# One change to a tuned kernel: the instruction order of its main region is left to the framework's scheduler

## The chip, the cores and the metric

The kernel runs on one core of a Trainium2 chip. The core has five engines that run side by side, each through its own list of instructions in the order of that list, and wait for one another on semaphores: PE (TensorE, matrix products), DVE (VectorE), ACT (ScalarE), POOL (GpSimd) and SP (SyncE, which here issues most of the DMA transfers). The metric is the device time of one execution in microseconds (us); lower is better. The kernel before took 1051.46 us, the median of three runs (1046.29 to 1054.59).

## The reference, cut to what matters

Three layers, one after the other, on 2304 tokens of 512 channels: block-causal attention, a gated feed-forward layer, and a layer of eight experts of which each token uses one.

```python
scores = scale * q @ k.T                          # 4 batches, 8 heads, 576 positions, 64 wide
scores = where(block_i >= block_j, scores, -1e9)  # blocks of 64 positions
attn   = exp(scores - max) / (sum + 1e-9)
x      = merge_heads(attn @ v)                    # 2304 x 512
x      = (sigmoid(x @ w_gate) * (x @ w_val)) @ w_out      # 512 -> 1536 -> 512, weights in float64
logits = x @ g                                    # 2304 x 8
e      = argmax(logits); p = softmax(logits)[e]
out    = p * (relu(x @ w1[e]) @ w2[e])            # per token, 512 -> 1024 -> 512
```

## The kernel before, in words

**Attention.** 4 batches x 4 pairs of heads x 5 query tiles make 80 items. An item goes through PE (scores L254 or L263/L270, masks L276), DVE (row maximum L291/L293), ACT (exp L307/L316), DVE (sum and reciprocal L324, L326, scaling L361), PE (transposes L338/L347 into `ep`), ACT (copy `et` L340), PE (times v, L383), ACT and DVE (the result `x` as a rounded part L391 and a rest L392) and POOL (store to `x_d`, L394). The letters of the strings G, H and QUICK give the order of these steps over neighbouring items. Batch 0 has a form of its own (`quick`), for which k and q are transposed on PE (L217) and copied by ACT and DVE to `qn` (L222) and `kn` (L224).

**Weights.** The feed-forward weights arrive as float64 and are turned on the chip into a rounded float32 part and a rest, in 27 pieces, of which 15 have 128x1024 elements. For each piece SP loads the words into one of three buffers (L556), ACT makes the exponent part (L568), DVE shifts and joins the words (L569, L573, and the add L578), ACT casts to the rounded part (L587) and DVE takes the rest (L589). `weights()` is a generator; before the feed-forward layer starts it is advanced by a pace (FILL) between the letters of the attention strings.

**Feed-forward.** Nine units `u` of 256 tokens, twelve blocks `f` of 128 columns. For each (u, f) PE forms gate and value in `gv` (L652 to L654, 24 matmuls of 256 columns), ACT and DVE form the product (`th` L677/L678, `g` L680/L681), and PE adds `g` times `w_out` to `acc` (L694). Unit u can start when its tokens' attention items have been stored and loaded again (`xu`). The work of units 0 and 1 runs interleaved with the attention of later batches and with the weight pieces; from unit 2 on the attention is fed in by a rate that counts how many steps are needed before the next unit.

**Routing and experts.** Logits are made per unit on PE (L718, L727, L737). The first 16 tiles of 128 tokens are routed while the last unit runs, the last two after it. Routing turns logits into a table of token numbers: matmuls into `pt` (L885), then on DVE `tb`, `ix` and `gi` (L898 to L902). The experts work in slots of 128 tokens: 9 early ones and then up to a total of 20 that are always executed. For a slot POOL gathers the tokens by `gi` (L1008, an indirect DMA), PE transposes them (L1031, `xtp`), ACT and DVE split them (`xt`, L1033/L1034). The expert's weights are four tiles `raw` of 1 MB, loaded by SP (L975/L977) and split by ACT into `eh` (L998) and by DVE into `el` (L999); PE multiplies (L1045, `hp` and `yp`), ACT applies relu and makes `h` (L1056), PE transposes it (L1065), ACT and DVE split it (`ht`, L1067/L1068), ACT scales the result by the gate (L1085) and POOL stores it to the rows of its tokens (L1086).

**What sets the order.** All this is emitted inside one region, `with tc.manual_schedule():` (L1096), in the order that the loops of the region give: the list `msegs` for the feed-forward layer, credits and paces for attention and weights, the strings TICK0 to TICK2 for the slots. In that region every engine gets its instructions in the order in which they are emitted.

Of the kernel before, what the change touches and what calls it, by code (L numbers as in the profile page):

```python
# [24 lines left out]
def attn_moe_moe_kernel(  # L25
# [1067 lines left out]
        )  # L1093


    with tc.manual_schedule():  # L1096
        ag = attention()
        done = [-3]

# [319 lines left out]
```

## Time and profile before

| | before |
|---|---|
| median of 3 runs | 1051.46 us |
| the profiled execution: its time | 1051.92 us |
| its span, first to last instruction | 1050.1 us |
| mean granted TensorE clock | 0.968 |
| PE busy | 957.8 us (91%) |
| DVE busy | 626.0 us (60%) |
| ACT busy | 578.2 us (55%) |
| POOL busy | 128.3 us (12%) |

The span is that of the core's instructions; 1.8 us of the execution lie around it. Busy times are sums over the whole span, and the stages differ: the table of stretches shows each engine's busy time in the part of the span named at the start of the row, with the granted clock of TensorE (1.00 is 2.4 GHz, 0.50 is 1.2 GHz). A wait belongs to the engine named first; behind the arrow stands what ended it.

### The profile page before, as it was taken

The numbers are of one execution on the slowest core, as the hardware profiler recorded it, in microseconds if no ns is written. First come the engines' busy times: TensorE is split into PE (matmuls) and PEld (weight loads), VectorE is DVE, ScalarE is ACT, GpSimd is POOL, SyncE is SP. The second block draws the span as 40 slices with busy tenths as digits, with TensorE's granted clock in tenths as the row PEclk, the third lists the DMA queues.
The fourth block names the chain that finished last, engine by engine and source line by source line (L and its number), as shares of the span: only waits on it lengthen the run. The fifth ranks groups of instructions, "written<-read, shape, count | busy, mean of one in ns | idle before, by whom it ended". The sixth has DMA issues, their size and how long they took to land. (4 is left out here: it accounts for less than half of the span.)

```text
span 1050.1 us, 17803 instructions
## 1 busy us (share of the span) xinstructions
PE 957.8 (91%) x6636; PEld 818.2 (78%) x6636; DVE 626.0 (60%) x1194; ACT 578.2 (55%) x1188; POOL 128.3 (12%) x180
## 2 busy tenths in 40 slices
PE   6776777997879999999999999999989999999994
PEld 3445676886658988888988998999987888888883
DVE  5777887765333444444444432121648999988984
ACT  5665565653534545445454532222238888888884
POOL 1211101111000110100101000000021123122110
PEclk9988989998999999999999999999999999999998
DMA  8546661422342031031130020201262354969110
GB/s 214 165 131 203 191 185 56 121 81 80 118 118 63 16 112 41 23 106 34 30 95 24 14 71 6 66 3 61 87 235 81 116 189 138 334 227 357 47 41 20
DMA packets 114715, 112.91 MB, mean 108 GB/s; under 512 B 62591, under 2 KB 85119, under 8 KB 114624
## 3 DMA queue, kind: packets, MB, share of 16 engines
q1 hardware_dynamic: 106800, 88.90, 27.6%
q0 software_dynamic: 7824, 22.82, 6.4%
q8 instruction: 54, 0.88, 0.3%
q14 instruction: 37, 0.30, 0.1%
HBM read 144.46 MB, written 22.28 MB: 159 GB/s over the span
## 5 line engine op out<-in xcount | busy, mean ns | idle before, releaser
L652 PE MATMUL gv<-xu,w 128*128 128x256 f32 x776 | 229.8, 296 | 6.5 <-ACT w L587 6.0
L653 PE MATMUL gv<-xu,w 128*128 128x256 f32 x776 | 220.6, 284 | 0.0
L654 PE MATMUL gv<-xu,w 128*128 128x256 f32 x776 | 220.6, 284 | 0.0
L999 DVE TENSOR_TENSOR el<-raw,eh 128x2048 fp32r<-128x2048 f32 x84 | 191.6, 2289 | 26.6 <-ACT eh L998 25.2
L694 PE MATMUL acc<-w,g 128*128 128x512 f32 x582 | 163.6, 410 | 4.6 <-ACT x2r L708 2.7
L998 ACT CAST eh<-raw 128x2048 fp32r<-128x2048 f32 x84 | 161.0, 1918 | 3.8 <-DMA raw<-in_moe_w_dram 3.7
L652 PEld LDWEIGHTS gv<-xu,w 128*128 128x128 f32 x776 | 149.6, 193 | 13.1 <-ACT w L587 6.5
L653 PEld LDWEIGHTS gv<-xu,w 128*128 128x128 f32 x776 | 149.7, 193 | 1.1
L654 PEld LDWEIGHTS gv<-xu,w 128*128 128x128 f32 x776 | 149.3, 192 | 0.0
L678 DVE SCALAR_TENSOR_TENSOR th<-th,gv 128x256 f32<-128x256 f32 x108 | 45.2, 418 | 143.4 <-ACT th L677 142.9
L694 PEld LDWEIGHTS acc<-w,g 128*128 128x128 f32 x582 | 102.3, 192 | 23.7 <-ACT x2r L708 3.2
L394 POOL DMA_DIRECT2D x_d<-x x80 | 54.8, 685 | 521.1 <-DVE x L392 350.1
L1045 PE MATMUL hp<-eh,xt 128*128 128x512 f32 x320 | 109.2, 402 | 0.0
L1045 PE MATMUL yp<-eh,ht 128*128 128x512 f32 x320 | 106.1, 393 | 0.7 <-ACT ht L1067 0.7
L677 ACT ACTIVATE th<-gv 128x256 f32<-128x256 f32 x108 | 41.6, 385 | 117.1 <-PE gv L654 116.9
L307 ACT ACTIVATE e<-sp,nm 128x128 f32<-128x128 f32 (+3 forms) x128 | 66.4, 526 | 50.8 <-DVE nm L291 50.5
L680 ACT CAST g<-th 128x256 fp32r<-128x256 f32 x108 | 43.9, 406 | 78.7 <-DVE th L678 75.8
L681 DVE TENSOR_TENSOR g<-th,g 128x256 fp32r<-128x256 f32 x108 | 45.9, 425 | 52.6 <-ACT g L680 52.6
L383 PE MATMUL av<-et,v 128*64 128x128 f32 (+1 forms) x960 | 67.6, 272 | 5.4 <-ACT et L340 5.1
L1045 PEld LDWEIGHTS yp<-eh,ht 128*128 128x128 f32 x320 | 59.9, 188 | 13.5 <-ACT ht L1067 0.9
L338 PE MATMUL ep<-ident,e 128*128 128x128 f32 x320 | 57.0, 285 | 14.5 <-DVE x L392 8.6
L1045 PEld LDWEIGHTS hp<-eh,xt 128*128 128x128 f32 x320 | 60.2, 188 | 11.9
(190 smaller groups left out, 1575.0 us busy)
## 6 DMA issues: line engine op xcount, KB each, us to landing
raw<-in_moe_w_dram SPq DMA_DIRECT2D x88, 1024.0 KB
xu<-x_d SPq DMA_DIRECT2D x36, 256.0 KB
x_d<-x POOLq DMA_DIRECT2D x64, 128.0 KB, 2.3
spare<-in_moe_w_gate_dram SPq DMA_DIRECT2D x10, 512.0 KB
spare<-in_moe_w_val_dram SPq DMA_DIRECT2D x10, 512.0 KB
spare<-in_moe_w_out_dram SPq DMA_DIRECT2D x10, 512.0 KB
x_d<-x2r SPq DMA_DIRECT2D x9, 512.0 KB
k<-in_k_dram SPq DMA_DIRECT2D x32, 128.0 KB
```

What stands on the lines that cost most here:

```text
L307: nc.scalar.activation(out=r["e"][:, j, 0:n], in_=r["view"][:, j, :], func=AF.Exp, bias=r["nm"][:, j:j + 1], accum_out=su[:, j:j + 1],)
L338: nc.tensor.transpose(ep[:, cs], r["e"][:, part, cs], ident)
L383: nc.tensor.matmul(av[hs, 0:m], lhsT=d["v"][:, c, j, :], rhs=rhs, start=(c == 0), stop=(c == t))
L394: nc.gpsimd.dma_start(out=x_d[hp][:, :, t0:t0 + m], in_=x[:, :, 0:m].bitcast(F32))
L652: nc.tensor.matmul(o, lhsT=wh, rhs=x[:, 0, :], start=(kk == 0 and nm == "g"), stop=False, **kw)
L653: nc.tensor.matmul(o, lhsT=wh, rhs=x[:, 1, :], start=False, stop=False, **kw)
L654: nc.tensor.matmul(o, lhsT=wl, rhs=x[:, 0, :], start=False, stop=(kk == KD - 1), **kw)
L681: nc.vector.tensor_tensor(out=g[:, 1, :], in0=th, in1=g[:, 0, :], op=ALU.subtract)
L694: nc.tensor.matmul(o, lhsT=g[:, part, hs], rhs=w_o(w, f), start=(f == fs[0] and w == "h" and part == 0), stop=(f == fs[-1] and part == 1),)
L998: nc.scalar.copy(out=h, in_=raw[j])
L999: nc.vector.tensor_tensor(out=l, in0=raw[j], in1=h, op=ALU.subtract)
L1045: nc.tensor.matmul(o, lhsT=t[:, cs], rhs=w[:, c * 512:(c + 1) * 512], start=(first and c == 0 and part == 0 and w is eh), stop=(last and c ...
```

## The change

One line. The region of fixed order becomes an empty context, and the framework's scheduler chooses the order of the instructions on every engine within what their data allow:

```diff
@@ -1093,7 +1093,7 @@
-    with tc.manual_schedule():
+    with ExitStack():
         ag = attention()
         done = [-3]
```

The instructions are the same ones in the same numbers on each engine, and no tile, buffer or transfer is added or removed. From about 300 to about 750 us PE's order is the same row for row. It differs at three places, which follow. Names are those of the tiles: what is written, an arrow, what is read; a trailing number tells instances of a tile apart (the numbers themselves differ by two between the kernels).

DVE at the start of the program. `kn` and `nm` belong to attention (keys, row maxima), `spare` is the buffer of weight pieces. Before:

```order
L224 COPY kn<-tp 128x576
L291 TENSOR_REDUCE nm<-sp 128x2
L324 TENSOR_SCALAR su<-su 128x2
L326 RECIPROCAL su<-su 128x2
L361 TENSOR_SCALAR e<-e,su 128x128 x2
L291 TENSOR_REDUCE nm<-sp 128x2
L324 TENSOR_SCALAR su<-su 128x2
L326 RECIPROCAL su<-su 128x2
L569 TENSOR_SCALAR spare_105<-spare_102 128x1024
```

Now:

```order
L569 TENSOR_SCALAR spare_105<-spare_102 128x1024
L224 COPY kn<-tp 128x576
L573 SCALAR_TENSOR_TENSOR spare_105<-spare_102,spare_105 128x1024
L578 ISA spare_105<-spare_105,spare_106 128x2048
L291 TENSOR_REDUCE nm<-sp 128x2
L569 TENSOR_SCALAR spare_105<-spare_103 128x1024
L291 TENSOR_REDUCE nm<-sp 128x2
L573 SCALAR_TENSOR_TENSOR spare_105<-spare_103,spare_105 128x1024
L324 TENSOR_SCALAR su<-su 128x2
L578 ISA spare_105<-spare_105,spare_106 128x2048
```

The rounding of weight pieces 0 and 1 moved ahead of the first key copy and the first maxima; on ACT, L568 of both pieces moved ahead of the first exp in the same way. By the 18th write of `x` DVE now has the instructions of about four more pieces in front of it (32 of them instead of 17); by the 24th write the two orders stand level.

PE in the third unit of the feed-forward layer, at the first use of the weights `w17`. Before:

```order
L338 MATMUL ep_2785<-ident_77,e_2698 128x128 x3
L652 MATMUL gv_2814<-xu_948,w17_2796 128x256
L653 MATMUL gv_2814<-xu_948,w17_2796 128x256
L654 MATMUL gv_2814<-xu_948,w17_2796 128x256
L652 MATMUL gv_2814<-xu_948,w17_2796 128x256
```

Now:

```order
L338 MATMUL ep_2783<-ident_77,e_2696 128x128 x3
L338 MATMUL ep_2825<-ident_77,e_2696 128x128 x3
L694 MATMUL acc_1231<-w16_2155,g_2723 128x512 x3
L270 MATMUL sp_2857<-ka_991,qa_989 128x288
L271 MATMUL sp_2857<-ka_991,ql_990 128x288
L270 MATMUL sp_2857<-ka_991,qa_989 128x288
L271 MATMUL sp_2857<-ka_991,ql_990 128x288
L270 MATMUL sp_2857<-ka_991,qa_989 128x288
L271 MATMUL sp_2857<-ka_991,ql_990 128x288
L270 MATMUL sp_2857<-ka_991,qa_989 128x288
L652 MATMUL gv_2812<-xu_946,w17_2794 128x256
```

Transposes, an `acc` part and scores that came behind this block's `gv` now stand ahead of it, and most of the block's other matmuls come 28 rows later.

DVE at the passage to the experts, where the token numbers `gi` of the first slots are made. Before:

```order
L999 TENSOR_TENSOR el_8376<-raw_7514,eh_8375 128x2048
L678 SCALAR_TENSOR_TENSOR th<-th,gv 128x256
L681 TENSOR_TENSOR g<-th,g 128x256
L898 COPY tb<-pt 128x45
L900 SCALAR_TENSOR_TENSOR ix<-tb 128x9
L901 TENSOR_SCALAR ix<-ix 128x9
L902 CAST gi<-ix 128x9
L904 TENSOR_SCALAR em<-tb 128x9
L905 TENSOR_TENSOR si<-em,ix 128x9
L906 TENSOR_TENSOR tb<-tb 128x9
L907 TENSOR_TENSOR gw<-tb 128x9
L999 TENSOR_TENSOR el_8441<-raw_7515,eh_8440 128x2048
```

Now:

```order
L999 TENSOR_TENSOR el_8439<-raw_7513,eh_8438 128x2048
L678 SCALAR_TENSOR_TENSOR th<-th,gv 128x256
L999 TENSOR_TENSOR el_8481<-raw_7514,eh_8480 128x2048
L681 TENSOR_TENSOR g<-th,g 128x256
L678 SCALAR_TENSOR_TENSOR th<-th,gv 128x256
L898 COPY tb<-pt 128x45
L900 SCALAR_TENSOR_TENSOR ix<-tb 128x9
L904 TENSOR_SCALAR em<-tb 128x9
L906 TENSOR_TENSOR tb<-tb 128x9
L901 TENSOR_SCALAR ix<-ix 128x9
L681 TENSOR_TENSOR g<-th,g 128x256
L902 CAST gi<-ix 128x9
```

The second and third `el` of slot 0 moved ahead of `gi`. In the slots that follow, ACT's `eh` and DVE's `el` of a slot come about one slot earlier than before, in the same cycle; SP's reads of slot numbers come earlier, in blocks.

## Rows read from the trace of the kernel before

**Rows 1.** Busy time by stretch: length, each engine's busy us (instructions), granted clock, DMA share, GB/s.

```profile
0.00:84.00 84.00, 61.34 (x472) 38.25 (x473) 58.64 (x138) 50.00 (x146) 15.01 (x34) 0.94 0.60 164
84.00:157.00 73.00, 52.76 (x386) 46.48 (x385) 59.38 (x109) 44.33 (x99) 7.41 (x15) 0.84 0.67 202
157.00:300.00 143.00, 119.06 (x870) 101.21 (x869) 83.46 (x218) 71.58 (x205) 17.72 (x32) 0.93 0.34 97
300.00:750.00 450.00, 443.73 (x3456) 397.29 (x3455) 174.76 (x486) 184.97 (x514) 30.43 (x59) 1.00 0.17 48
750.00:800.00 50.00, 44.87 (x296) 39.52 (x296) 29.88 (x58) 24.81 (x34) 6.01 (x4) 0.97 0.57 200
```

**Rows 2.** The same view, two stretches of the early slots.

```profile
800.00:850.00 50.00, 50.00 (x246) 41.32 (x245) 47.85 (x67) 43.09 (x42) 10.97 (x8) 1.00 0.36 127
850.00:900.00 50.00, 50.00 (x259) 41.39 (x258) 49.13 (x46) 42.23 (x41) 16.06 (x8) 1.00 0.44 151
```

**Rows 3.** DVE in order of time, start of the program: start, us, engine, line, tiles.

```profile
5.64 0.76 DVE L224 COPY kn<-tp 128x576 f32<-128x576 f32 x1 [4.39 <-ACT qn L222]
9.47 0.42 DVE L291 TENSOR_REDUCE nm<-sp 128x2 f32<-128x256 f32 x1 [3.07 <-PE sp L276]
```

**Rows 4.** ACT in order of time, start of the program.

```profile
7.77 0.60 ACT L222 ACTIVATE qn<-tp 128x512 f32<-128x512 f32 x1 [2.16 <-PE tp L217]
...
13.50 1.17 ACT L568 ACTIVATE spare<-spare 128x1024 int32<-128x1024 uint32 x1
```

**Rows 5.** SP's issues in order of time, start of the program.

```profile
4.96 0.51 SPq L556 DMA_DIRECT2D spare<-in_moe_w_val_dram  x1
```

**Rows 6.** DMA of the first 16 us, the line of totals.

```profile
DMA packets 7536, 3.62 MB, mean 226 GB/s; under 512 B 6256, under 2 KB 7280, under 8 KB 7536
```

**Rows 7.** DVE by line and shape, 0 to 84 us: tiles, count, busy, mean ns.

```profile
L573 DVE SCALAR_TENSOR_TENSOR spare<-spare,spare 128x1024 int32<-128x1024 int32 x5 | 6.1, 1218 | 0.0
...
L589 DVE TENSOR_TENSOR w<-spare,w 128x1024 fp32r<-128x1024 f32 x4 | 4.9, 1216 | 0.0
L578 DVE CUSTOM_DVE_ANT_0 spare<-spare,spare 128x2048 uint16<-128x2048 uint16 x4 | 4.8, 1212 | 0.0
...
L569 DVE TENSOR_SCALAR spare<-spare 128x1024 int32<-128x1024 int32 x5 | 3.5, 705 | 0.0
```

**Rows 8.** PE in order of time, first matmul of the feed-forward layer.

```profile
84.01 0.36 PE L652 MATMUL gv<-xu,w 128*128 128x256 f32 x1
```

**Rows 9.** PE's waits, 100 to 350 us: us in total, times, longest.

```profile
PE gv L652 <- ACT w L587: 6.0, 2, 3.9
```

**Rows 10.** PE in order of time, work behind the `gv` of w17.

```profile
259.86 0.86 PE L694 MATMUL acc<-w,g 128*128 128x512 f32 x3
...
261.70 0.88 PE L383 MATMUL av<-et,v 128*64 128x128 f32 x12
```

**Rows 11.** DVE in order of time, passage to the experts.

```profile
761.95 2.29 DVE L999 TENSOR_TENSOR el<-raw,eh 128x2048 fp32r<-128x2048 f32 x1 [0.24 <-ACT eh L998]
...
766.03 0.17 DVE L902 CAST gi<-ix 128x9 uint32<-128x9 f32 x1
...
766.86 2.29 DVE L999 TENSOR_TENSOR el<-raw,eh 128x2048 fp32r<-128x2048 f32 x1
```

**Rows 12.** POOL in order of time, the first gathers.

```profile
767.14 2.98 POOL L1008 DMA_INDIRECT xs<-x_d,gi  x1 [82.01 <-DMA raw<-in_moe_w_dram]
777.72 1.03 POOL L1008 DMA_INDIRECT xs<-x_d,gi  x1 [7.60 <-PE gv L654]
```

**Rows 13.** PE in order of time, the first transpose of gathered tokens.

```profile
775.08 1.08 PE L1031 MATMUL xtp<-ident,xs 128*128 128x128 f32 x4 [2.97 <-DMA xs<-x_d,gi]
```

**Rows 14.** PE's waits, 740 to 800 us.

```profile
PE xtp L1031 <- ACT lt L730: 1.0, 1, 1.0
```

**Rows 15.** DVE by line and shape, 788 to 900 us.

```profile
L999 DVE TENSOR_TENSOR el<-raw,eh 128x2048 fp32r<-128x2048 f32 x36 | 81.7, 2285 | 10.1 <-ACT eh L998 9.9
```

**Rows 16.** ACT in order of time, a cast that waits for its weights.

```profile
869.41 1.92 ACT L998 CAST eh<-raw 128x2048 fp32r<-128x2048 f32 x1 [1.50 <-DMA raw<-in_moe_w_dram]
```

## The prediction

> **What bounds the kernel now.** I read the busy times by stretch first, then the waits, then each engine in order of time at the places where the order changes. The stretches show one bound with holes in it: PE. It is busy for 443.73 of the 450 us from 300 to 750 and for all 100 us of the two stretches of early slots, at full clock [rows 1, 2]; there a new order of DVE or ACT gains nothing and can only lose. PE's idle time lies in four places: 84.00 - 61.34 = 22.7 us up to the first feed-forward matmul at 84.01 [rows 8], 20.2 us from there to 157, 23.9 us from 157 to 300, and 5.1 us in the passage to the experts [rows 1]. In the first two the granted clock is 0.94 and 0.84, and DVE is as busy as PE or busier (58.64 of 84, 59.38 of 73), so the start is a chain through PE, ACT and DVE in which no engine is full. The order of PE is the same from 300 to 750, so the change can pay or cost at three places only: up to 300, at the passage (750 to 815), and in the slots, if PE loses its cover there.
>
> **The change part by part.** The sum goes against the profiled execution, 1051.92 us (span 1050.1, 1.8 us around it); that is 0.5 us over the median of 1051.46, so the two are taken as one.
>
> *The start.* DVE now rounds weights before the first key copy. The words of pieces 0 and 1 must land first. The later of the first two loads is issued at 4.96 [rows 5]; 1.05 MB for the pair at the 226 GB/s of the first 16 us [rows 6] is 4.6 us, so an estimate for the landing is 4.96 + 0.51 + 4.6 = 10.1; L568 at 13.50 without a wait bounds it from above [rows 4]. The key copy, at 5.64 before [rows 3], comes behind L569 (0.70 us [rows 7]) at about 10.8. L573 and L578 (1.22 and 1.21 us) stand between it and the first maximum: 10.8 + 0.76 + 2.43 = 14.0 instead of 9.47, or 4.5 us late. On ACT the large query copy, at 7.77 before [rows 4], comes behind one L568 (1.17 us) at about 11.3; that is inside the same delay. By the 18th `x`, which releases the first feed-forward matmul, DVE has fifteen more rounding instructions in front: 4 x 0.70 + 3 x 1.22 + 4 x 1.21 + 4 x 1.22 = 16.2 us. DVE has 84.00 - 58.64 = 25.4 us idle in this stretch, most of it in short waits within the chain, so some of the 16.2 goes into holes. The first feed-forward matmul is then late by 4.5 (everything but the first delay hidden) to 16.2 us (nothing hidden). I take 9, near the middle, since the chain of an item passes DVE five times and each pass can meet a 1.2 us instruction.
>
> *From there to 157.* By the 24th `x` the orders are level, so DVE's 59.38 us in this stretch shrink to about 59.38 - 16.2 = 43.2. Starting at 84 + 9 = 93: if PE's own 52.76 us [rows 1] are the limit, the meeting point comes at 145.8, 11 us early. If DVE keeps its 73.00 - 59.38 = 13.6 us of idle time, it comes at 93 + 43.2 + 13.6 = 149.8, 7 us early. If the stretch keeps its 73 us (its attention items still pass engine after engine), it comes at 166, 9 us late. These are the ends, -11 and +9. The row that speaks of this stretch itself has neither PE nor DVE full, so I take a value between the second and the third case, and put the two pieces together at **-2 us**.
>
> *157 to 300.* The orders stay close, with one visible exception: PE's two waits for the cast of w17, 6.0 us [rows 9]. Now an `acc` part, a set of scores and av work stand ahead of that block. From the start of the `acc` part at 259.86 to the start of av is 1.84 us, av is 0.88 [rows 10], together 2.7. So between 0 (the cast is late by the same amount, or these rows are not ready) and -6 (further transposes that were moved as well fill the rest); I take **-3 us**.
>
> *The passage.* `gi` is written at 766.03 before [rows 11]. Now the second and third `el` come ahead of it, 2 x 2.29 = 4.6 us, at about 770.6. Behind `gi`, POOL's first gather takes 2.98 us before and the second 1.03 [rows 12]; an `el` began at 766.86, 0.28 us ahead of the first, and filled most of it. In the new order no `el` stands right behind `gi`, so I price the new gather at 1.03, 2.0 us less. The transposes that wait for it, at 775.08 after a wait of 2.97 us [rows 13], move by 4.6 - 2.0 = 2.6 us, and PE's place in its order has not moved, so the 2.6 us are PE's. The Trainium skill, page "SBUF — State Buffer", section "SBUF: two separate sides", says that a VectorE operation with two operands in SBUF and a GpSimd operation that reads SBUF hold a shared port one at a time, the later one blocked until the first is done. The trace agrees in that the slow gather is the one begun under an `el`; without this rule the gather would keep 2.98 and the passage would cost 2.0 us more. Against it, router work that PE waited for now has a slot's second product in front of it, and a wait of 1.0 us goes [rows 14]. Together **+2 us** (0 if the three `el` run in DVE's idle time, 50.00 - 29.88 = 20 us in this stretch; +8 if a late `el` also holds back the `g` behind it and PE's `acc` with it).
>
> *The slots.* `eh` and `el` move one slot earlier, in the same cycle. That is four extra `el`, 4 x 2.29 = 9.1 us of DVE [rows 15], to be found once. The early slots have 50.00 - 47.85 + 50.00 - 49.13 = 3.0 us to spare on DVE [rows 2], the passage some 20. I put this at **0**, covered by the passage. If that cover is missing, PE waits for `ht` or `xt` (the third rival). SP's earlier reads of slot numbers lie in SP's waits for DVE: 0.
>
> The sum: -2 - 3 + 2 + 0 = -3, so 1051.9 - 3 = **1049 us**.
>
> **The rivals.**
>
> *A, the holes at the start fill.* The feed-forward work is no longer short of weights, and 84 to 157 runs at PE's own work. For it: DVE has 16.2 us less to do there, and a denser PE would also leave the clock above 0.84. Against it: PE's order, with its attention steps, is nearly unchanged. First part -11, w17 -6, passage 0: 1051.9 - 17 = 1035 us.
>
> *B, slower: the attention chain stays behind.* What is lost by the first feed-forward matmul is not won back, since every later unit needs attention items that come off the same chain. The place is DVE from 0 to 157; it decides if the chain's 73 us after that matmul do not shrink. For it: each engine takes its list in order, and a weight instruction whose words are not there (three buffers, of which the loads share 226 GB/s with k, q and v) holds the maxima behind it. Against it: 25.4 us of idle DVE. First part +9, w17 0, passage +3: 1064 us.
>
> *C, slower: the slots lose their cover.* ACT's casts of 1.92 us now come a slot early; one that waits for its `raw` tile, as at 869.41 for 1.50 us [rows 16], holds `ht` behind it, and PE needs `ht` for the next product. If each of seven early slots lost one cast, 7 x 1.92 = 13.4 us: 1049 + 13 = 1062 us. Against it: PE has no wait at all in these slots before, with ACT at 43.09 and 42.23 of 50, so a short one is absorbed.
>
> **How the numbers follow.** The forecast has 0.45, with a range of its own of 1041 to 1060 (the first part from -8 to +6, the others within their ends); A 0.22, B 0.17, C 0.16. The predicted time is 1049. The range that should hold the time 8 times in 10 reaches to A and to just past B: 1035 to 1066; half of A and a few of B and C are left out. A measurement can tell about 1% from no change, so faster is below 1041 and slower above 1062. Faster: A and a little of the forecast's low tail, 0.25. Slower: B, over half of C and a little of the forecast's high tail, 0.32. The same: 0.43.
>
> **What would show it.** The start: the first maximum at about 14, the first feed-forward matmul at about 93 (between 88 and 100). The next part: the unit after it begins at most a few us from its old time; PE's idle time from 84 to 300 falls from 44 us to under 40. w17: waits for L587 of about 3 us rather than 6. The passage: `gi` near 771 (less any earlier shift), the first gather near 1 us, PE's wait for it 5 to 6 us. The slots: PE busy at 50 of 50. It is wrong if PE waits for `ht`, `xt` or `eh` in the slots, if the w17 wait only moves to another row, or if the units from 300 on begin more than 10 us from their old times.

## The result, and the profile after

The changed kernel takes 1000.48 us (median of 3 runs, 996.51 to 1009.91) against 1051.46. The ratio is 0.9539, 95% interval 0.9417 to 0.9660: 51 us less where 2.5 less were forecast, and outside the range of 1035 to 1066. The profiled execution has a span of 998.4 us and a mean granted clock of 0.993 (0.968 before).

The page of the changed kernel, part 1:

```profile
PE 950.1 (95%) x6636; PEld 807.8 (81%) x6636; DVE 607.7 (61%) x1194; ACT 580.8 (58%) x1188; POOL 136.7 (14%) x180
```

PE is busy for 950.1 us instead of 957.8, and idle for 998.4 - 950.1 = 48.3 us instead of 1050.1 - 957.8 = 92.3. So 44.0 us of the gain in span are idle time, and 7.7 us are less busy time of the same matmuls. The clock alone does not account for the second part: of the runs below, the one with only the feed-forward loop free has 944.1 us of PE busy at a mean clock of 0.988, and the one with only PE free 978.1 at 0.976. The stretches of the changed kernel, as in [rows 1]:

```profile
0.00:84.00 84.00, 64.75 (x448) 37.44 (x448) 65.08 (x146) 56.69 (x150) 16.74 (x35) 1.00 0.84 243
84.00:157.00 73.00, 70.12 (x574) 61.69 (x574) 66.74 (x147) 53.28 (x133) 11.74 (x21) 1.00 0.46 135
157.00:300.00 143.00, 139.32 (x1078) 118.62 (x1077) 79.89 (x231) 80.83 (x235) 18.01 (x33) 1.00 0.38 108
```

From 84 to 157 PE is busy for 70.12 of 73 us, against 52.76, with a granted clock of 1.00 against 0.84; from 157 to 300 for 139.32 of 143, against 119.06. DVE does more in the first of the two (66.74 against 59.38 us) and PE nevertheless waits less for it. In PE's waits from 84 to 300 of the changed kernel (total us, times, longest), the three largest are

```profile
PE gv L652 <- DMA xu<-x_d: 2.8, 3, 1.1
PE sp L263 <- ACT e L307: 0.8, 1, 0.8
PE ep L338 <- ACT et L340: 0.7, 1, 0.7
```

The w17 wait of [rows 9] is gone, and the others that PE had between 100 and 350 in the kernel before are gone or under 1 us in total (`gl` 0.6). Three more of those before are these:

```profile
PE ep L338 <- DVE x L392: 8.6, 4, 3.9
...
PE tp L217 <- ACT e L316: 5.2, 2, 4.1
PE acc L694 <- DMA gl<-g_d: 4.9, 2, 3.9
```

How far the attention has come is read from DVE's writes of `x` (L392) in order of time; the time at which the n-th starts, with the median times of the runs:

| kernel | time, us | 1st x | 18th | 25th | 45th |
|---|---|---|---|---|---|
| before | 1051.5 | 16.0 | 82.6 | 156.8 | 330.9 |
| the change | 1000.5 | 23.4 | 86.2 | 134.4 | 278.9 |

The changed kernel is 7.4 us behind at the 1st, 3.6 behind at the 18th, 22.4 ahead at the 25th and 52.0 ahead at the 45th: the whole gain lies between 86 and 280 us. After that the lead hardly changes: it is 51.7 us at the end of the span.

The orders differ more than the description of the change says. It names three places, but when each instruction is paired with its twin in the other trace, at least 50 of DVE's 107 instructions from 84 to 157 and 79 of 217 from 157 to 300 would have to be moved to turn one list into the other; of PE's matmuls it is 55 of 383 and 115 of 868. From 300 to 750 PE's order is nearly the same and not wholly (22 of 3455).

### The profile page after: what moved, and what is told of

Same layout as the page of the kernel before. It is cut to its first block, busy times and chain, and to the rows that moved or that the text cites. A ratio compares the mean times of both kernels' runs of the same rounds, so it can differ in the third digit from the quotient of the medians.

```text
span 998.4 us, 17867 instructions
## 1 busy us (share of the span) xinstructions
PE 950.1 (95%) x6636; PEld 807.8 (81%) x6636; DVE 607.7 (61%) x1194; ACT 580.8 (58%) x1188; POOL 136.7 (14%) x180
## 5 line engine op out<-in xcount | busy, mean ns | idle before, releaser
L652 PEld LDWEIGHTS gv<-xu,w 128*128 128x128 f32 x776 | 147.9, 191 | 9.7 <-issue 4.1
L653 PEld LDWEIGHTS gv<-xu,w 128*128 128x128 f32 x776 | 148.0, 191 | 1.3
L654 PEld LDWEIGHTS gv<-xu,w 128*128 128x128 f32 x776 | 147.8, 190 | 0.5 <-issue 0.2
L678 DVE SCALAR_TENSOR_TENSOR th<-th,gv 128x256 f32<-128x256 f32 x108 | 45.2, 418 | 138.0 <-ACT th L677 137.7
L307 ACT ACTIVATE e<-sp,nm 128x128 f32<-128x128 f32 (+3 forms) x128 | 66.6, 527 | 22.4 <-DVE nm L291 21.3
L1045 PEld LDWEIGHTS yp<-eh,ht 128*128 128x128 f32 x320 | 60.4, 190 | 17.1 <-ACT y L1085 3.6
L383 PE MATMUL av<-et,v 128*64 128x128 f32 (+1 forms) x960 | 69.2, 267 | 3.6 <-ACT et L345 2.0
L340 ACT COPY et<-ep 128x128 f32<-128x128 f32 (+3 forms) x128 | 53.0, 427 | 32.1 <-PE ep L338 30.8
L383 PEld LDWEIGHTS av<-et,v 128*64 128x64 f32 x960 | 47.5, 137 | 25.8 <-ACT et L340 6.7
L680 ACT CAST g<-th 128x256 fp32r<-128x256 f32 x108 | 44.0, 408 | 39.3 <-DVE th L678 34.3
```

Of the source, the lines that this page charges most:

```text
L307: nc.scalar.activation(out=r["e"][:, j, 0:n], in_=r["view"][:, j, :], func=AF.Exp, bias=r["nm"][:, j:j + 1], accum_out=su[:, j:j + 1],)
L340: nc.scalar.copy(out=et[:, 0:w], in_=ep[:, 0:w])
L383: nc.tensor.matmul(av[hs, 0:m], lhsT=d["v"][:, c, j, :], rhs=rhs, start=(c == 0), stop=(c == t))
L652: nc.tensor.matmul(o, lhsT=wh, rhs=x[:, 0, :], start=(kk == 0 and nm == "g"), stop=False, **kw)
L653: nc.tensor.matmul(o, lhsT=wh, rhs=x[:, 1, :], start=False, stop=False, **kw)
L654: nc.tensor.matmul(o, lhsT=wl, rhs=x[:, 0, :], start=False, stop=(kk == KD - 1), **kw)
```

## The experiments

All are compared with the kernel before on the same chip (median 1050.2 to 1050.8 us in each group). The engines' names in the diffs are those of the language; `Activation` is ACT.

**Whose order.** Five runs fix the order of some engines as it was before and leave the others to the scheduler. The first fixes PE:

```diff
-    with tc.manual_schedule():
+    with tc.manual_schedule(engines={mybir.EngineType.PE}):
```

> PE's instructions keep the fixed order of before; the scheduler orders DVE, ACT, POOL and SP. If the gain of 51 us comes from the order of DVE and ACT (weight pieces ahead, short steps that PE waits for taken first), this keeps most of it: 1000 to 1015 us. If it comes from PE's own order, whose list no longer stops at a row that is not ready, this is near before: 1035 to 1055 us.

Measured 1028.22 us, ratio 0.980 (0.9773 to 0.9827). Neither end holds: 22 of 51 us without any change of PE's order.

The complement, `engines={Activation, DVE, Pool, SP}` fixed:

> The complement: DVE, ACT, POOL and SP keep the fixed order of before, the scheduler orders PE alone. If the gain is PE's own order: 1000 to 1020 us. If it is the order of DVE and ACT: 1040 to 1060 us. If both are needed, this and the run with PE fixed both stay above 1025 us.

Measured 1045.93 us, ratio 0.9957 (0.9930 to 0.9984). PE's order alone gives 4.3 us. The third case holds, both runs stay above 1025 us: 22 and 4.3 make 26.3 and not 51.

`engines={DVE}` fixed:

> DVE alone keeps the fixed order of before, the scheduler orders the others. DVE is the busiest engine beside PE from 84 to 157. If DVE's order (row maxima and sums behind weight rounding of 1.2 us each) is what holds the chain, nearly all of the gain goes: 1035 to 1050 us. If ACT's and PE's orders carry it, most stays: 1005 to 1020 us.

Measured 1045.24 us, ratio 0.9944 (0.9922 to 0.9966). The first case: freeing PE, ACT, POOL and SP together is worth 5.5 us as long as DVE's list stands.

`engines={Activation}` fixed:

> ACT alone keeps the fixed order of before. If ACT's order (casts that wait for DVE's join or for th, with exps and copies for PE behind them) is what holds the chain: 1035 to 1050 us. If DVE's is: 1005 to 1020 us. If each of the two is enough to hold the others to its pace, both runs stay above 1030 us.

Measured 1014.88 us, ratio 0.9640 (0.9609 to 0.9671). ACT's order is the least of the three: 36 us of the gain come without it. The stretch from 84 to 157 with DVE fixed, and then with ACT fixed:

```profile
84.00:157.00 73.00, 55.26 (x403) 45.89 (x404) 56.88 (x103) 43.85 (x100) 8.56 (x17) 0.87 0.54 161
```

```profile
84.00:157.00 73.00, 61.66 (x462) 50.51 (x461) 62.06 (x119) 50.67 (x117) 9.88 (x19) 0.95 0.60 183
```

PE is busy for 55.26 and for 61.66 us, at a clock of 0.87 and 0.95; before, it was 52.76 at 0.84.

Only DVE free, `engines={PE, Activation, Pool, SP}` fixed:

> Only DVE is ordered by the scheduler; PE, ACT, POOL and SP keep the fixed order of before. With DVE fixed 45 of the 51 us are lost, so DVE's order is needed. If it is enough: 1005 to 1025 us. If the lists of ACT and PE then hold DVE to the old pace: 1035 to 1050 us.

Measured 1032.89 us, ratio 0.9837 (0.9794 to 0.9879): 17.5 us, between its cases. So DVE's order is needed for nearly all of the gain and is enough for a third of it. The runs make a ladder: PE 4.3, DVE 17.5, DVE with ACT 22, DVE with PE 36, all 50 us. POOL and SP are free in every one of these but the first two, and no run frees them by themselves; with DVE alone fixed they were free too, and 5.5 us came.

What each list does to an attention item is read from the traces by pairing the n-th row maximum (L291/L293) with the n-th product with v (L383) and the n-th `x` (L392). Mean times of the 19th to the 25th item, in us:

| kernel | row maximum to first product with v | last product with v to x | row maximum to x | the same, 26th to 45th |
|---|---|---|---|---|
| before | 16.7 | 3.9 | 21.6 | 18.9 |
| only DVE free | 16.6 | 2.9 | 20.6 | 17.8 |
| DVE fixed | 9.5 | 10.3 | 21.1 | 17.1 |
| PE fixed | 14.6 | 1.3 | 16.8 | 16.2 |
| ACT fixed | 14.0 | 4.5 | 20.6 | 16.6 |
| the change | 10.7 | 2.0 | 14.0 | 14.6 |

With DVE alone free, the way up to the product with v is as long as before. With DVE fixed it is short, but the time won is lost again in front of `x`, which stands in DVE's list. The change has both ways short. The times follow the gain only roughly (ACT fixed gains more than PE fixed), so they show a part of the cause and not all of it. Before and in the change about two items are on this way at a time (mean from 84 to 157 us 2.1 and 2.0): the items are faster, there are not more of them at once.

**Which stretch.** The region is cut in parts, each fixed or free for all engines, by entering and leaving the fixed order at the loop's boundaries:

```diff
-    with tc.manual_schedule():
+    man = [None]
+    def fixed_order(on):
+        if man[0] is not None:
+            man[0].__exit__(None, None, None)
+        man[0] = tc.manual_schedule() if on else None
+        if on:
+            man[0].__enter__()
+    with ExitStack():
+        fixed_order(False)        # start
...
+        fixed_order(True)         # ahead of the feed-forward loop
...
+        fixed_order(True)         # ahead of the slots
```

Only the start free, as shown:

> The scheduler has all engines only in the part of the program that is emitted before the feed-forward loop (17 items of attention and the first weight pieces); from there the order is fixed as before. If the weight pieces that were put ahead at the start are the cause: 1005 to 1025 us. If the cause lies in the loop, in which attention, weights and feed-forward are interleaved: 1045 to 1060 us, for the first 84 us alone the start came out 4 us later.

Measured 1049.03 us, ratio 0.9985 (0.9968 to 1.0002): nothing. The 18th x came at 81.3 us, the 25th at 153.2.

Only the feed-forward loop free:

> The scheduler has all engines only in the feed-forward loop; the start and the slots are fixed as before. If the cause lies in the loop: 1000 to 1020 us. If it is the weight pieces ahead at the start: 1035 to 1055 us.

Measured 1006.29 us, ratio 0.9585 (0.9563 to 0.9607): 44 us, the first case.

The loop cut at the first block of unit 2, only units 0 and 1 free:

> The scheduler has all engines only in the part of the feed-forward loop that is emitted for units 0 and 1, where weight pieces, attention and feed-forward are interleaved; start, units 2 to 8 and slots are fixed as before. If the weight rounding between the attention steps is where the holes come from, this keeps most of the 44 us that freeing the whole loop gave: 1010 to 1020 us. If the holes are as much those of attention against feed-forward in the units after, it keeps about half: 1022 to 1035 us.

Measured 1012.77 us, ratio 0.9640 (0.9609 to 0.9671), the first case: 37 us.

Only the loop from unit 2 on free:

> The complement: start, units 0 and 1 fixed, the scheduler has the loop from unit 2 on. First case: 1035 to 1050 us. Second case: 1022 to 1035 us. The two gains should add up to about 44 us if they are independent.

Measured 1029.54 us, ratio 0.9804 (0.9768 to 0.9839): 21 us, the second case. 37 and 21 make 58, more than the 44 of both: what the first part wins, the second finds in part already won. The start is fixed in these runs, and the last instruction (L589) of the 8th weight piece began at 112.7 us in the run with units 0 and 1 free (119.1 before, 92.6 in the change), so the gain of 37 us needs no weight pieces ahead of the loop.

The change with the slots fixed:

> The change, with the slots of the experts (and the late routing between them) in the fixed order of before. In the profile of the changed kernel PE waits some 4 to 6 us in the slots, where it had no wait before. If that is the price of the slots' new order, this is 4 to 6 us faster than the change: 994 to 997 us. If PE waits there because the whole chain came earlier, it is the same: 999 to 1003 us.

Measured 1001.36 us (993.39 to 1005.06), ratio 0.9515 (0.9457 to 0.9573), not to be told from the change. What the slots' order costs is below this resolution.

The change with the first five attention items fixed (the region is left when the item with index 2 has been emitted):

> The change, with the first five attention items in the fixed order of before, which keeps the first weight pieces behind the first key copy and maxima. In the changed kernel the first x comes 7.4 us later than before. If this delay is passed on to the end: 993 to 997 us. If PE wins it back, since it is short of weights next: 999 to 1003 us.

Measured 1000.02 us, ratio 0.9524 (0.9466 to 0.9583): the second case. The first x came at 16.8 us, 6.5 us before that of the change, and the 25th at 135.2, 0.8 us behind it. A delay at the start is won back.

**What in the order.** By hand, in fixed order, the activation is split:

```diff
         nc.vector.scalar_tensor_tensor(out=th, ...)
-        g = mw.tile(...)
-        nc.scalar.copy(out=g[:, 0, :], in_=th)
-        nc.vector.tensor_tensor(out=g[:, 1, :], in0=th, in1=g[:, 0, :], op=ALU.subtract)
-        gts[u, f] = g
+        def second():
+            g = mw.tile(...)
+            nc.scalar.copy(out=g[:, 0, :], in_=th)
+            nc.vector.tensor_tensor(out=g[:, 1, :], in0=th, in1=g[:, 0, :], op=ALU.subtract)
+            gts[u, f] = g
...
+        later.append([2, second])   # emitted two steps of msegs later
```

> Fixed order throughout, with one edit by hand: of each feed-forward block's activation the second half (the cast g on ACT and the rest on DVE) is emitted two steps of the loop after the first half (th), so that other work stands between the four hops ACT, DVE, ACT, DVE. ACT waits 25.9 us for DVE's th and DVE 11.4 us for ACT's g between 84 and 300 in the kernel before, 4.2 and 4.1 us in the changed one. If these hops are the main part of what the scheduler removes: 1015 to 1035 us. If they lie beside other waits: 1045 to 1055 us.

Measured 1042.31 us, ratio 0.9921 (0.9893 to 0.9948): 8 us, between the two cases. ACT's wait for `th` from 84 to 300, in the kernel before, the changed one, and this one (total us, times, longest; L683 and L679 are L680 and L678 here), with its wait for PE's product with v in the kernel before and in this one:

```profile
ACT g L680 <- DVE th L678: 25.9, 24, 2.8
...
ACT x L391 <- PE av L383: 6.8, 5, 2.5
```

```profile
ACT g L680 <- DVE th L678: 4.2, 10, 0.5
```

```profile
ACT x L391 <- PE av L383: 17.9, 7, 8.0
...
ACT g L683 <- DVE th L679: 2.5, 5, 0.9
```

The wait went from 25.9 to 2.5 us, lower than the scheduler's 4.2, and a sixth of the gain came with it. Other waits took its place: ACT's for `av` rose from 6.8 to 17.9 us, and all of ACT's waits listed for this stretch add up to 96.6 us instead of 92.7.

Weight pieces ahead by hand:

```diff
-    FILL = 0.35
+    FILL = 1.0
```

> Fixed order throughout, with the pace of the weight generator in the start raised from 0.35 to 1.0 steps per letter, so that weight pieces are rounded ahead of the feed-forward loop by hand. If the gain is that the feed-forward layer is no longer short of weights (the rival A of the prediction): 1010 to 1035 us. If weights ahead are no use as long as the loop's lists stop at every step that is not ready: 1045 to 1060 us.

Measured 1043.36 us, ratio 0.9934 (0.9908 to 0.9961): 7 us, just under its second case, far from the first. The last instruction (L589) of the 8th piece began at 69.8 us instead of 119.1, and the 18th x came at 101.9 instead of 82.6. From there the 25th x took 54.2 us instead of 74.2 (156.1 against 156.8): weights ahead made this stretch 20 us shorter, and rounding them had made the start 19 us longer. So the 7 us are not what weights in time would be worth if they cost the start nothing.

Both hand edits:

> Fixed order with both hand edits: weight pieces ahead by a pace of 1.0 and the second half of the activation two steps later. Alone they measured -7.4 and -7.9 us. If they act on different holes: 1033 to 1038 us; if on the same ones: 1040 to 1045 us; if one opens the way for the other, as with DVE's and PE's order: under 1030 us.

Measured 1041.18 us, ratio 0.9924 (0.9895 to 0.9953): the second case, 9 us where the two alone add up to 15, so they act in good part on the same holes.

Two instructions per weight piece left out, in fixed order and in the scheduler's (each measured once; the weights, the routing and what follows are then other values, so only the time up to the 45th x is read):

```diff
         elif stage == 1:
-            nc.vector.scalar_tensor_tensor(out=b, in0=w1, ...)      # L573
             wread[0] = n
         else:
-            nc.vector.tensor_tensor(out=b, in0=b, in1=r, op=ALU.add)  # L578
+            pass
```

> Fixed order as before, with two of DVE's four instructions per weight piece left out (L573 and the add L578), so the feed-forward weights are wrong and so are the routing and everything after it; the time of the start and of the feed-forward loop is what counts. That is 15 x 2.43 = 36 us of DVE work less before about 180 us. If the rounding bunched on DVE in front of the attention's steps makes the holes: the 45th x comes at 285 to 305 us instead of 330.9. If it is the order itself, with lists that stop at steps that are not ready: 315 to 328 us.

> The same two instructions left out (weights, routing and all after wrong), with the scheduler's order on all engines. In the changed kernel the 45th x comes at 278.9 us and PE is busy for 70 of 73 us from 84 to 157. If bunched rounding is what the scheduler dissolves, the work left out is of little use here: 270 to 279 us, and the fixed and the free kernel come within 20 us of each other. If the order itself decides, they stay 35 us or more apart.

The two stretches, fixed and then free:

```profile
84.00:157.00 73.00, 61.41 (x467) 55.11 (x467) 51.11 (x111) 50.75 (x115) 8.90 (x16) 0.91 0.66 201
157.00:300.00 143.00, 124.21 (x937) 104.38 (x935) 68.53 (x189) 73.68 (x212) 17.00 (x31) 0.98 0.38 106
```

```profile
84.00:157.00 73.00, 69.06 (x557) 59.79 (x555) 53.97 (x140) 57.48 (x151) 12.68 (x24) 0.98 0.61 192
157.00:300.00 143.00, 140.56 (x1096) 119.96 (x1096) 71.70 (x197) 76.97 (x220) 17.75 (x33) 1.00 0.34 95
```

The 45th x came at 304.7 us fixed and at 283.2 free. Taking 36 us of work from DVE is worth 26 us in fixed order, at the upper edge of the first case, and nothing in the free one (278.9 with the work). But the two stay 21.5 us apart, and with DVE at 51.11 of 73 us PE is still busy for only 61.41 in fixed order, and for 69.06 with a DVE as lightly loaded (53.97) in free order. The free run fits neither of its cases: 283.2 us is later than 270 to 279, and 21.5 us lies between 20 and 35. So about half of the lead at the 45th x (52 us) answers to the rounding work in DVE's list, and about 20 us are left to the order with that work taken out.

How that looks in DVE's list is shown by the two kernels at a similar place, after the 20th x. Before, in order of time:

```profile
106.07 1.22 DVE L573 SCALAR_TENSOR_TENSOR spare<-spare,spare 128x1024 int32<-128x1024 int32 x1
107.20 1.22 DVE L589 TENSOR_TENSOR w<-spare,w 128x1024 fp32r<-128x1024 f32 x1
108.46 0.69 DVE L569 TENSOR_SCALAR spare<-spare 128x1024 int32<-128x1024 int32 x1
109.07 1.22 DVE L578 CUSTOM_DVE_ANT_0 spare<-spare,spare 128x2048 uint16<-128x2048 uint16 x1
110.30 0.17 DVE L290 MEMSET sp<- 64x128 f32 x1
110.50 0.96 DVE L291 TENSOR_REDUCE nm<-sp 128x2 f32<-128x768 f32 x1
111.38 1.22 DVE L573 SCALAR_TENSOR_TENSOR spare<-spare,spare 128x1024 int32<-128x1024 int32 x1
112.51 0.28 DVE L392 TENSOR_TENSOR x<-av,x 128x128 fp32r<-128x128 f32 x1
```

The change:

```profile
97.26 1.22 DVE L573 SCALAR_TENSOR_TENSOR spare<-spare,spare 128x1024 int32<-128x1024 int32 x1
98.39 0.15 DVE L326 RECIPROCAL su<-su 128x2 f32<-128x2 f32 x1
98.57 0.17 DVE L290 MEMSET sp<- 64x128 f32 x1
98.65 0.42 DVE L361 TENSOR_SCALAR e<-e,su 128x128 f32<-128x128 f32 x2
98.98 0.68 DVE L291 TENSOR_REDUCE nm<-sp 128x2 f32<-128x512 f32 x1
99.58 1.22 DVE L589 TENSOR_TENSOR w<-spare,w 128x1024 fp32r<-128x1024 f32 x1
101.72 0.17 DVE L324 TENSOR_SCALAR su<-su 128x2 f32<-128x2 f32 x1 [0.92 <-ACT e L307]
101.80 1.22 DVE L578 CUSTOM_DVE_ANT_0 spare<-spare,spare 128x2048 uint16<-128x2048 uint16 x1
```

Before, four rounding instructions stand in one block of 4.2 us between the `th`/`g` pair of a feed-forward block and the next maximum (L291), and a fifth ahead of `x`. In these rows of the change each rounding instruction stands alone between short steps of two attention items (sums, reciprocals, scalings, maxima). Over all of the 108 rounding instructions 64 stand alone instead of 41, and DVE's blocks of four or more are one instead of five. That this spacing is what PE profits from is my reading and not shown. It is not enough by itself: with only DVE free the rounding was as spaced (60 alone, one block of four or more), and 17.5 us came. A kernel that spaces the rounding by hand within the loop was not tried.

## Why the prediction was wrong, step by step

**The bound.** Right: PE from 300 on, nothing to gain there, and the holes between 0 and 300 as the only ones large enough. The 66.8 us of idle time summed there were the gain's ceiling, apart from what PE's busy time can itself lose.

**The first maximum.** Right: the loads landed in time for L569 at 10.47 (estimate 10.1), and the first maximum came at 14.74 (14.0). DVE at the start of the changed kernel:

```profile
10.47 0.69 DVE L569 TENSOR_SCALAR spare<-spare 128x1024 int32<-128x1024 int32 x1 [9.22 <-DMA spare<-in_moe_w_val_dram]
...
14.74 0.42 DVE L291 TENSOR_REDUCE nm<-sp 128x2 f32<-128x256 f32 x1 [0.41 <-PE sp L276]
```

**The first feed-forward matmul.** Predicted 9 us late, between 4.5 and 16.2. It came 2.8 us late (84.01 in [rows 8]):

```profile
86.84 0.36 PE L652 MATMUL gv<-xu,w 128*128 128x256 f32 x1
```

Even the low end was too high. I took the first delay as the least that must arrive, but it shrank from 7.4 us at the 1st x to 3.6 at the 18th. DVE's idle time (84.00 - 65.08 = 18.9 us now, 25.4 before) took up the added work and, as I read it, part of the delay. The run with the first items fixed shows the rest of it to be without price.

**From there to 157.** This is the step that failed: -2 us put between ends of -11 and +9. From the first feed-forward matmul to the 25th x it took 134.38 - 86.84 = 47.5 us instead of 72.7, with nearly the same number of matmuls; this part before and now:

```profile
84.01:156.75 72.74, 52.50 (x384) 46.22 (x382) 59.12 (x106) 44.32 (x99) 7.39 (x15) 0.84 0.67 202
```

```profile
86.84:134.38 47.54, 45.57 (x387) 40.38 (x385) 42.48 (x90) 35.15 (x87) 7.24 (x13) 1.00 0.59 170
```

PE's idle time here went from 20.2 to 2.0 us. The end of -11 used PE's 52.76 us as a floor, but those are us at a granted clock of 0.84; now the clock was 1.00 and PE's busy time 45.57. And between the ends I chose the value because attention items "still pass engine after engine". They do, about two at a time as before, but an item now takes 14.0 us from its row maximum to its `x` instead of 21.6. DVE, which I had as busy as PE, could give more in this time: 66.74 us in the 73.

**157 to 300.** The same failure, and larger: -3 us predicted, 52.0 - 22.4 = 29.6 measured. I judged the orders "close", with w17 as the one visible exception. They were not (79 of DVE's 217 instructions here moved against the others), and small moves counted: freeing the loop from unit 2 on alone is worth 21 us. The w17 wait went wholly, at my end of -6.

**The passage.** `gi` behind two more `el`, and the gather at 1.03 us, were both as predicted; DVE, POOL and PE at the passage of the changed kernel, each in order of time:

```profile
702.59 2.29 DVE L999 TENSOR_TENSOR el<-raw,eh 128x2048 fp32r<-128x2048 f32 x1 [2.50 <-ACT eh L998]
...
711.79 0.17 DVE L902 CAST gi<-ix 128x9 uint32<-128x9 f32 x1
...
722.25 2.29 DVE L999 TENSOR_TENSOR el<-raw,eh 128x2048 fp32r<-128x2048 f32 x1 [1.09 <-ACT eh L998]
```

```profile
712.88 1.09 POOL L1008 DMA_INDIRECT xs<-x_d,gi  x1 [83.80 <-DVE gw L907]
720.48 1.03 POOL L1008 DMA_INDIRECT xs<-x_d,gi  x1 [6.50 <-PE gv L654]
721.81 1.00 POOL L1008 DMA_INDIRECT xs<-x_d,gi  x1 [0.30 <-PE gv L654]
723.12 2.30 POOL L1008 DMA_INDIRECT xs<-x_d,gi  x1 [0.30 <-issue]
```

```profile
718.83 0.66 PE L1031 MATMUL xtp<-ident,xs 128*128 128x128 f32 x4 [0.69 <-DMA xs<-x_d,gi]
```

The first gather took 1.09 us. But PE waited for it only 0.69 us, not 5 to 6. That "PE's place in its order has not moved" was not enough: the group of `el` ahead of `gi` had itself come earlier against PE, and its first now began 16.2 us before the transposes (702.59, 718.83), where the only one ahead of `gi` had begun 13.1 us before them ([rows 11, 13]).

**The slots.** Predicted 0. PE now has small holes there, seen in the waits from 720 to 970 and in the stretches:

```profile
PE yp L1045 <- ACT y L1085: 3.2, 1, 3.2
...
PE htp L1065 <- ACT h L1056: 0.8, 1, 0.8
```

```profile
700.00:750.00 50.00, 47.41 (x305) 40.39 (x304) 32.14 (x39) 32.85 (x41) 7.96 (x6) 1.00 0.52 184
750.00:800.00 50.00, 50.00 (x247) 41.27 (x246) 48.62 (x69) 45.17 (x42) 14.99 (x9) 1.00 0.49 161
800.00:850.00 50.00, 48.08 (x249) 39.37 (x247) 46.37 (x41) 40.07 (x37) 13.37 (x7) 1.00 0.62 218
850.00:950.00 100.00, 97.95 (x472) 81.49 (x473) 88.07 (x57) 86.09 (x83) 22.78 (x16) 0.98 0.52 185
```

From 750 to 950 PE lacks 1.9 + 2.1 = 4.0 us. The largest wait, 3.2 us for `y`, was not followed further. One of the smaller ones is rival C in small: a cast that waits for its weights, with `h` behind it on ACT, after which PE waits 0.8 us for `h`:

```profile
811.23 1.91 ACT L998 CAST eh<-raw 128x2048 fp32r<-128x2048 f32 x1 [1.22 <-DMA raw<-in_moe_w_dram]
813.04 0.59 ACT L1056 ACTIVATE h<-hp 128x512 f32<-128x512 f32 x1
```

With the slots' order fixed the time was the same within its interval, so no price of this is shown.

**The rivals.** A had the right sign and place, priced at 17 us where 51 came. Its reason, that the feed-forward layer is short of weights, is not the main one: freeing units 0 and 1 alone gave 37 us with the 8th piece only 6.4 us earlier. Weights ahead by hand gave 7 us, but that run also paid for them at the start. B, the lost start that is not won back, is refuted by the change itself, 22.4 us ahead at the 25th x, and the run with the first items fixed shows that the start's delay cost nothing. The passage and the slots together, +2 us in the sum, cost 52.0 - 51.7 = 0.3 us, within their ends.

No run beats the change: with the slots or the first items fixed it comes to 1001.4 and 1000.0 us, the same. DVE's and PE's orders give 17.5 and 4.3 us alone and 36 together (with POOL's and SP's), so about 14 us need both. The table of the items shows where: up to the product with v and in front of `x`. Which instructions make it so stays open.

## What to carry to other kernels

Where three engines pass short steps to one another and none is full, price a new order against the idle time of the engine that sets the end, and not only by the few waits that it can be seen to remove. Here 44 of 92 us of PE's idle time went, where I had priced the visible waits at a few us. Find whose list holds the chain by fixing one engine's order at a time: here the busy helper's (DVE) was needed for 45 of 50 us, though PE sets the end. Then follow one item of the chain through the engines: an order can be quick in one part of the way and lose it in the next. Removing one wait by hand, from 25.9 to 2.5 us, gave a sixth, and other waits grew by as much.

## What the runs showed of the hardware

From 84 to 157 us PE's granted clock was 0.84 with 20.2 us idle and 1.00, which is 2.4 GHz, with 2.9 us idle. Idle time does not give the clock by itself: in the first 84 us it was 0.94 with 22.7 us idle, and 1.00 with 84.00 - 64.75 = 19.3 us idle.

POOL's gathers bear out what the first one suggested: one that began 0.87 us into an `el` of DVE (722.25 to 724.54) took 2.30 us, the one at 720.48, with no `el` beside it, 1.03. The Trainium skill's rule of the shared port (page "SBUF — State Buffer", section "SBUF: two separate sides") fits the gathers of both kernels. The other direction of the rule is not seen here: this `el` began 0.44 us into the gather at 721.81, which took 1.00 us, and it took its usual 2.29.
